# Low-rank attention and a maxout layer on one core: two heads of q fetched beside k, with E and F behind them, and batch 0's scores put ahead of v's projection

## The chip, the core and the metric

The kernel runs on one core of a Trainium2 chip. A core has a matrix engine (TensorE, PE in the profile), a vector engine (VectorE, DVE), an activation engine (ScalarE, ACT), a general engine (GpSimd, POOL) and a sequencer that issues transfers (SyncE, SP). Sixteen DMA engines move data between the chip's main memory (HBM) and the on-chip memory. A transfer is issued on a queue: SP's and ScalarE's are hardware queues, POOL's is a software queue. In this kernel every transfer that turns float32 into float16 on its way is on POOL's queue. TensorE writes into eight banks of accumulator memory (PSUM), and VectorE and ScalarE copy from there.

The metric is the device time of one execution in microseconds.

## The reference

The inputs are q, k and v with 8 batches, 8 heads, 1024 positions and 64 features per head, all float32; E and F, 64 by 1024; and three weight matrices. Keys and values are first projected from 1024 positions to 64:

```python
k_proj = np.einsum('ks,bhsd->bhkd', E, k)
v_proj = np.einsum('ks,bhsd->bhkd', F, v)
scores = (1.0 / np.sqrt(64)) * np.matmul(q, k_proj.transpose(0, 1, 3, 2))
attn = softmax(scores)                     # over the 64 projected keys
x = np.matmul(attn, v_proj)                # then heads side by side: 8192 x 512
h1 = x @ w1                                # 512 x 1024
h2 = x @ w2
out = np.maximum(h1, h2) @ w_out           # 1024 x 512, float32
```

The kernel computes the maximum as a ReLU of `x @ (w1 - w2)` plus `x @ w2`, and folds `w2 @ w_out` into one matrix m.

## The kernel before

**Steady state.** A batch is handled in two halves of its positions (`units`, 16 in all). For batches 1 to 7 the large products are done by a scheme with seven block products in place of eight (`up_steps`, L693, and `down_steps`, L785), with the sums and differences of blocks made on VectorE. The attention of a later batch is woven between them. All of it is an order written out by hand: a list `slots` of closures, and a table `steps` that hangs further closures on slots. The framework adds the semaphores and, under `manual_schedule`, leaves the order as written: each engine works through its own instructions in program order, so an instruction that waits holds up all behind it on the same engine.

**The beginning, where the change is.** Before that list, batch 0 is handled by straight-line code (L897 to L943), and the transfers for it are issued at the top:

- SP's queue: E (L80), the first two heads of k uncast in float32 (`kf_sb`, L81), F (L82). E and F share `ef_sb`.
- POOL's queue, in float16: heads 2 and 3 of k, then q's heads 0 to 3, k's 4 to 7, q's 4 to 7 (the double loop around L112), v in four pairs of heads (L117), then the weights w1 and w2 in pieces (L124, L133) and w_out (L137). The identity matrix is made on POOL after the first of them.
- `kf_sb` lies in the buffer that w_out takes later (tag `wo`). VectorE casts head 0 from it (L901) and ScalarE head 1 (L902).

The steps of batch 0, in the order that TensorE gets them: `step_eft` transposes E or F (L161, eight float32 transposes) and copies the result to `eft` (L167). `step_kv` projects k or v (L187): k four heads at a time into `kp`, v two or four heads at a time into `vp`. `step_kpt` transposes the projected k (L277). `step_qt` transposes four heads of q for one half of the positions (L303) and VectorE copies them (L308). `step_sc` makes the scores of a group of four heads (`g`) and a half (`j`) with 16 matmuls (L332), and ScalarE takes the exponential (L372). `step_dn` sums the exponentials with a matmul by ones (L344) and ScalarE takes the logarithm (L380); `step_inv` turns it into the reciprocal (L384). `step_at` multiplies by the projected v (L344 again) and VectorE scales the result into `xt` (L399). `step_wd` makes `w1 - w2` (L495). Then the first `up` products of batch 0 follow (L479), and from there the list of slots.

Between these steps stand `warm(n)`: n dummy matmuls of 128x512 ones (L147) whose results nobody reads.

`mm_bank()` hands out four PSUM banks in rotation unless a bank is named, and every `warm`, `step_kv`, `step_qt` and so on takes the next; `att_banks()` hands out two pairs of banks. The seven block products that make m (`m_steps`, L581) name banks 2 and 3 for themselves, at the end of batch 0's `up`, and `p5` there keeps a sum in bank 3.

Of the kernel before, what the change touches and what calls it, by code (L numbers as in the profile page):

```python
# [8 lines left out]
FP32 = mybir.dt.float32  # L9
# [7 lines left out]
def kernel(  # L17
# [12 lines left out]
    nc = tc.nc  # L30
# [5 lines left out]
    NC = S // 128  # L36
# [36 lines left out]
    def big(n, dtype=FP16):  # L73
        return const.tile([128, 16384 // mybir.dt.size(dtype) // 2], dtype, tag=f"big{n}", name=f"big{n}")

    ef_sb = big(0, FP32)[0:KP, :].rearrange("k (i s) -> k i s", i=2)
    kf_sb = const.tile([128, 2048], FP32, tag="wo", name="kf_sb")[:, 0 : 2 * NC * D].rearrange(
        "p (h c d) -> p h c d", h=2, d=D
    )
    nc.sync.dma_start(out=ef_sb[:, 0, :], in_=E)  # L80
    nc.sync.dma_start(out=kf_sb, in_=k[0, 0:2].rearrange("h (p c) d -> p h c d", c=NC))  # L81
    nc.sync.dma_start(out=ef_sb[:, 1, :], in_=F)  # L82
    nc.scalar.add_instruction(
        mybir.InstLoadActFuncSet(
# [16 lines left out]
    def load(t, n, src, b, h0, h1):  # L101
        nc.gpsimd.dma_start(  # L102
            out=t[n][:, h0:h1],
            in_=src[b, h0:h1].rearrange("h (p c) d -> p h c d", c=NC),
        )
# [3 lines left out]
        alloc(tiles[0], n)  # L109
    for h0 in (0, H // 2):  # L110
        for n, src in (("k", k), ("q", q)):
            load(tiles[0], n, src, 0, h0 + 2 * ((h0, n) == (0, "k")), h0 + H // 2)  # L112
            if (h0, n) == (0, "k"):
                ident = const.tile([128, 128], FP32)
                make_identity(nc, ident)
# [28 lines left out]
    def warm(n, att=False):  # L144
        w_ps = att_banks()[:, 0, :] if att else mm_bank()
        for _ in range(n):
            nc.tensor.matmul(  # L147
                out=w_ps, lhsT=ones16[:, 0:128], rhs=ones16, start=True, stop=True
            )

    warm(8)
    ident16 = const.tile([128, 128], FP16)
    nc.vector.tensor_copy(out=ident16, in_=ident)

# [3 lines left out]
    def step_eft(i):  # L158
        eft_ps = mm_bank()
        for c in range(NC):  # L160
            nc.tensor.transpose(  # L161
                out=eft_ps[:, c * KP : (c + 1) * KP],
                in_=ef_sb[:, i].rearrange("k (p c) -> k c p", c=NC)[:, c, :],
                identity=ident[:KP, :KP],
            )
        eng = nc.scalar.copy if i else nc.vector.tensor_copy
        eng(out=eft[i].rearrange("p c k -> p (c k)"), in_=eft_ps)  # L167
# [9 lines left out]
    def step_kv(t, h0=0, h1=H, which="kv", att=False, dma=False, copy=nc.vector.tensor_copy):  # L177
        kv_ps = att_banks()[:, 0, :] if att else mm_bank(n=0 if dma else None)
        n = (h1 - h0) * D
        both = which == "v"  # L180
        nh = 2 if both else h1 - h0
        for h in range(0, h1 - h0, nh):
            for c in range(NC):
                for w in which:
                    i = "kv".index(w)
                    for r in range(2) if both else (i,):
                        nc.tensor.matmul(  # L187
                            out=kv_ps[r * KP : (r + 1) * KP, h * D : (h + nh) * D],
                            lhsT=eft[i][:, c, :],
                            rhs=t[w][:, h0 + h : h0 + h + nh, c, :],  # L190
                            start=(c == 0), stop=(c == NC - 1),
                        )
        zd = lambda ap: ap.rearrange("p (h d z) -> p h z d", d=D // 2, z=2)
        if "k" in which:
            eng = nc.vector.tensor_copy if which == "k" or dma else nc.scalar.copy
            kp = t["kp"][:, h0:h1]
            eng(out=kp[:, :, 0, :], in_=kv_ps[0:KP, 0:n].rearrange("p (h d) -> p h d", d=D))
        if both:
            copy(out=t["vp"][:, h0:h1], in_=zd(kv_ps[:, 0:n]))
        elif "v" in which:  # L200
            def finish_v():
                nc.vector.tensor_copy(out=t["vp"][KP:128, h0:h1], in_=zd(kv_ps[KP:128, 0:n]))
                if dma:
                    nc.vector.tensor_copy(out=kp[:, :, 1, :], in_=kp[:, :, 0, :])
                    step_kpt_dma(t)
                else:
                    step_vp(t, h0, h1)

            if att:
                return finish_v  # L210
            finish_v()
# [149 lines left out]
    def new_xt(t):  # L361
        t["xt"] = xpool.tile([128, NP2, 2, HALF], FP16, tag="xt", name="xt_sb")
# [5 lines left out]
    def step_sc(t, g, j):  # L368
        sc_ps = att_banks()
        t["ps", g, j] = sc_ps  # L370
        score(t, g, j, [sc_ps[:, e, :] for e in range(2)])
        nc.scalar.activation(out=t["ex", g, j], in_=sc_ps, func=ACTF.Exp, scale=scale)  # L372

    def step_dn(t, g, j):
        dn_ps = t.pop(("ps", g, j))[:, :, 0:W]
        sums_into(t, g, j, dn_ps)
        ld = (ppool.tile([128, 2, W], FP32, tag="pd", bufs=4, name="ld_sb") if t is tiles[0]
              else soft.tile([128, 2, W], FP32, tag="soft", name="ld_sb"))
        t["ld", g, j] = ld
        nc.scalar.activation(out=t["ld", g, j], in_=dn_ps, func=ACTF.Ln)  # L380

    def step_inv(t, g, j):
        ld = t["ld", g, j]
        nc.scalar.activation(out=ld, in_=ld, func=ACTF.Exp, scale=-1.0)  # L384
# [178 lines left out]
    def m_steps():  # L563
        st = {}
        two = lambda ap: ap.rearrange("q (i m) -> q i m", i=2)

        def product(k, name, n):
            if n is not None:
                st[name] = mm_bank(n=n)
            bank = st[name]  # L570
            Bb = lambda h, c: wo_sb[:, h * NG : (h + 1) * NG, c * CH : (c + 1) * CH]
            T = lambda i: T_sb[:, i, 0:NG, :]
            a, w_ = {
                1: lambda: (m_blk(0, 0), Bb(0, 0)), 2: lambda: (m_blk(0, 1), Bb(1, 0)),
                3: lambda: (m_sums[3], Bb(1, 1)), 4: lambda: (m_blk(1, 1), T(3)),
                5: lambda: (m_sums[0], T(0)), 6: lambda: (m_sums[1], T(1)),
                7: lambda: (m_sums[2], T(2)),
            }[k]()
            for i in range(2):
                for c in range(NG):  # L580
                    nc.tensor.matmul(  # L581
                        out=bank[:, i * CH : (i + 1) * CH],
                        lhsT=a[:, c, i * 128 : (i + 1) * 128],
                        rhs=w_[:, c, :],
                        start=(n is not None and i == 0 and c == 0),
                        stop=(c == NG - 1), skip_group_check=True,
                    )
            return bank

        def block(j, c):  # L590
            return m_sb[:, 2 * j : 2 * j + 2, c * CH : (c + 1) * CH]

        def add(j, c, x, y):
            nc.vector.tensor_tensor(out=block(j, c), in0=two(x), in1=two(y), op=ALU.add)

        def p1():
            st["s1"] = keep("pu", product(1, "X", 2))

        def p2():
            add(0, 0, product(2, "Y", 3), st["s1"])  # L600

        def p6():
            st["u1"] = keep("pu", product(6, "X", None))

        def p5():
            st["s5"] = keep("pu", product(5, "Z", 3))

        def p7():
            st["u2"] = keep("pu", product(7, "X", None))

        def p3():
            add(0, 1, product(3, "Z", None), st["u1"])
            add(1, 1, st["u2"], st["s5"])

        def p4():
            nc.scalar.copy(out=block(1, 0), in_=two(product(4, "X", None)))

        return [p1, p2, p6, p5, p7, p3, p4]
# [46 lines left out]
    def keep(tag, bank, copy=nc.scalar.copy):  # L665
        x = ppool.tile([128, 512], FP32, tag=tag, bufs={"pu": 3, "pd": 4}[tag], name="p_sb")
        copy(out=x, in_=bank)  # L667
        return x
# [228 lines left out]
    t = tiles[0]  # L897
    new_attn(t)
    new_xt(t)
    step_eft(0)  # L900
    nc.vector.tensor_copy(out=t["k"][:, 0], in_=kf_sb[:, 0])  # L901
    nc.scalar.copy(out=t["k"][:, 1], in_=kf_sb[:, 1])  # L902
    warm(5)
    step_kv(t, 0, 4, "k")
    step_eft(1)
    step_kpt(t, 0, 4)
    warm(3)
    step_qt(t, 0, 4, 0, NI // 2)
    step_qt(t, 0, 4, NI // 2, NI)
    warm(2)  # L910
    step_sc(t, 0, 0)
    step_sc(t, 0, 1)
    warm(2)
    step_kv(t, 4, 8, "k")
    step_dn(t, 0, 0)
    warm(2)
# [1 line left out]
    step_dn(t, 0, 1)  # L918
    step_inv(t, 0, 0)
    step_inv(t, 0, 1)  # L920
    warm(2)
    step_qt(t, 4, 4, 0, NI // 2)
    step_qt(t, 4, 4, NI // 2, NI)
    warm(2)
    step_sc(t, 1, 0)
    step_kv(t, 0, 2, "v")
    step_sc(t, 1, 1)
    step_kv(t, 2, 4, "v")
    step_dn(t, 1, 0)
    step_dn(t, 1, 1)  # L930
    step_inv(t, 1, 0)
    step_inv(t, 1, 1)
    step_at(t, 0, 0)
    step_at(t, 0, 1, between=lambda: step_wd(0, 0, 2))
    step_kv(t, 4, 8, "v", True, copy=nc.scalar.copy)
    step_at(t, 1, 0, True)
    u0, u1 = [*up_slots(t, 0)], [*up_slots(t, 1)]
    step_wd(0, 2, 4)
# [207 lines left out]
```

## Time and profile before

| what | value |
|---|---|
| median of 3 runs | 320.87 us (320.71 to 320.96) |
| the profiled execution | 321.09 us, span 319.3 us |
| TensorE busy | 312.9 us, 98% of the span |
| VectorE busy | 241.3 us, 76% |
| ScalarE busy | 205.8 us, 64% |
| GpSimd busy | 39.7 us, 12% |
| TensorE busy in 1.40 to 24.00 us | 20.80 of 22.60 us |
| TensorE busy in 24.00 to 45.00 us | 20.94 of 21.00 us |
| TensorE busy in 45.00 to 100.00 us | 54.90 of 55.00 us |
| TensorE busy in 100.00 to 314.00 us | 214.00 of 214.00 us |
| first `up` product (L479) begins | 23.48 us |

The span runs from the first to the last instruction; the device time has some 1.8 us around it. A line of the timeline gives the start, the duration, the engine, the source line, the operation, what is written from what, how many instructions were merged into the line, and in square brackets how long the engine had been idle before it and what ended that. A line of the chain of waits gives start, duration, and what the end of the program waited for in that stretch. A line of a DMA queue gives packets, megabytes written and the time that the packets took, as a share of sixteen engines over the stretch. Dummy matmuls count as busy time of TensorE.

### The profile page before, as it was taken

To read this page: it belongs to the slowest core of one execution; us is meant where nothing else is said; L and a number is where in the kernel's file an instruction comes from. 1 tells how busy PE (TensorE), PEld (TensorE's weight loads), DVE (VectorE), ACT (ScalarE), POOL (GpSimd) and SP (SyncE) were. 2 spreads that over 40 slices of the span, in tenths; PEclk is the share of its full clock that TensorE was granted. 3 is DMA by queue.
4 is the path that set the end of the run, shared out by engine and by line. 5 is a ranking of instruction groups with operands and counts; after the bars stand their busy time and mean duration, and the time that the engine had idled before them with its cause. 6 is when DMAs were issued, how large, how long until landed. Compare 5 with 4: busy or idle time off the path is not lost.

```text
span 319.3 us, 9176 instructions
## 1 busy us (share of the span) xinstructions
PE 312.9 (98%) x3920; PEld 253.2 (79%) x3920; DVE 241.3 (76%) x434; ACT 205.8 (64%) x372; POOL 39.7 (12%) x63
## 2 busy tenths in 40 slices
PE   8989999999999999999999999999999999999996
PEld 3554588788887888788887888788887888888885
DVE  2356889787969696896969696996969696969683
ACT  2376742767776777477776777477776777765541
POOL 8269102003000300021000400030000000000000
PEclk9999999999999999999999999999999999999999
DMA  7999999999979899899999999889969231303124
GB/s 185 200 200 193 199 207 202 207 165 154 206 136 179 156 205 245 219 192 158 233 204 215 168 216 245 198 157 169 239 141 211 50 102 35 101 33 102 35 99 131
DMA packets 76424, 53.41 MB, mean 167 GB/s; under 512 B 29536, under 2 KB 76000, under 8 KB 76384
## 3 DMA queue, kind: packets, MB, share of 16 engines
q0 software_dynamic: 30688, 28.05, 56.2%
q1 hardware_dynamic: 45408, 24.58, 32.3%
q8 instruction: 30, 0.49, 0.6%
q10 hardware_dynamic: 288, 0.20, 0.2%
q14 instruction: 10, 0.08, 0.1%
HBM read 57.15 MB, written 16.78 MB: 232 GB/s over the span
## 4 chain that ended last, share of the span: by engine, by line
PE 92%; DMA 4%; ACT 1%; POOL 1%; DVE 1%; issue 0%; POOLq 0%; DVEq 0%
PE mm_ps L785 46%; PE mm_ps L693 27%; PE mm_ps L479 4%; DMA v_sb<-in_v_dram 4%; PE att_ps L344 3%; PE mm_ps L187 3%; PE mm_ps L332 3%; PE mm_ps L581 2%; PE att_ps L229 1%; PE mm_ps L303 1%; POOL k_sb L102 0%; POOL q_sb L102 0%; PE att_ps L504 0%; PE att_ps L332 0%; ACT ld_sb L384 0%
## 5 line engine op out<-in xcount | busy, mean ns | idle before, releaser
L667 ACT COPY p_sb<-mm_ps 128x512 f32<-128x512 f32 x179 | 101.7, 592 | 49.4 <-PE mm_ps L693 27.3
L785 PEld LDWEIGHTS <-big 128*128 128x128 f16 x768 | 73.5, 98 | 11.8 <-issue 3.6
L785 PE MATMUL mm_ps<-T_sb,big 128*128 128x256 f16 x576 | 77.0, 273 | 0.0
L708 DVE TENSOR_TENSOR gt_sb<-mm_ps,p_sb 128x512 f16<-128x512 f32 x56 | 38.5, 687 | 42.7 <-PE mm_ps L693 42.3
L693 PE MATMUL mm_ps<-big,big 128*128 128x256 f16 x336 | 50.4, 273 | 0.0
L693 PEld LDWEIGHTS <-big 128*128 128x128 f16 x448 | 43.8, 98 | 5.1
L785 PE MATMUL mm_ps<-wo_sb,gt_sb 128*128 128x256 f16 x256 | 42.8, 273 | 0.0
L785 PEld LDWEIGHTS <-gt_sb 128*128 128x128 f16 x376 | 35.6, 98 | 7.0 <-issue 3.0
L425 ACT ACTIVATE ex_sb<-mm_ps 128x512 f16<-128x512 f32 x50 | 27.2, 596 | 18.2 <-PE mm_ps L332 13.0
L693 PEld LDWEIGHTS <-wd_sb 128*128 128x128 f16 x336 | 32.9, 98 | 4.1
L693 PE MATMUL mm_ps<-xt_sb,wd_sb 128*128 128x256 f16 x224 | 33.0, 272 | 0.0
L454 DVE TENSOR_TENSOR xt_sb<-att_ps,ld_sb 128x1024 f16<-128x1024 f32 x26 | 31.7, 1218 | 0.2
L785 PE MATMUL mm_ps<-m_sb,xt_sb 128*128 128x256 f16 x128 | 24.4, 273 | 0.0
L711 DVE TENSOR_SCALAR gt_sb<-gt_sb 128x512 f16<-128x512 f16 (+1 forms) x60 | 22.7, 378 | 2.1
L815 DVE TENSOR_TENSOR o_sb<-mm_ps,p_sb 128x512 f32<-128x512 f32 x32 | 21.8, 682 | 2.8 <-ACT p_sb L839 2.0
L295 POOL COPY junk<-qt_sb 1x1 f16<-1x1 f16 x6 | 1.1, 177 | 176.2 <-DMA qt_sb<-q_sb 176.2
L653 DVE TENSOR_TENSOR big<-gt_sb 128x1024 f16<-128x1024 f16 x32 | 21.9, 683 | 0.0
L785 PE MATMUL mm_ps<-wo_sb,big 128*128 128x256 f16 x128 | 21.5, 273 | 0.0
L754 ACT ACTIVATE gt_sb<-mm_ps 128x512 f16<-128x512 f32 x28 | 16.8, 601 | 5.7 <-PE mm_ps L693 5.7
L785 PE MATMUL mm_ps<-T_sb,gt_sb 128*128 128x256 f16 x120 | 20.3, 273 | 0.0
L785 PEld LDWEIGHTS <-xt_sb 128*128 128x128 f16 x188 | 18.4, 98 | 2.1
L708 DVE TENSOR_TENSOR gt_sb<-p_sb 128x512 f16<-128x512 f32 x28 | 19.1, 682 | 0.7 <-ACT p_sb L667 0.6
(112 smaller groups left out, 434.7 us busy)
## 6 DMA issues: line engine op xcount, KB each, us to landing
out_dram<-o_sb SPq DMA_DIRECT2D x62, 256.0 KB, 2.7
k_sb<-in_k_dram POOLq DMA_DIRECT2D x7, 1024.0 KB, 10.4
v_sb<-in_v_dram POOLq DMA_DIRECT2D x7, 1024.0 KB, 17.0
q_sb<-in_q_dram POOLq DMA_DIRECT2D x5, 1024.0 KB, 23.9
q_sb<-in_q_dram POOLq DMA_DIRECT2D x6, 512.0 KB, 16.2
big<-in_moe_w_dram POOLq DMA_DIRECT2D x12, 128.0 KB, 6.3
v_sb<-in_v_dram POOLq DMA_DIRECT2D x4, 256.0 KB, 13.8
wo_sb<-in_moe_w_out_dram POOLq DMA_DIRECT2D x1, 1024.0 KB, 10.4
```

The lines of the kernel that those rows point to most:

```text
L187: nc.tensor.matmul(out=kv_ps[r * KP : (r + 1) * KP, h * D : (h + nh) * D], lhsT=eft[i][:, c, :], rhs=t[w][:, h0 + h : h0 + h + nh, c, :], ...
L425: nc.scalar.activation(out=t["ex", g, j][:, e, :], in_=banks[e], func=ACTF.Exp, scale=scale)
L454: nc.vector.tensor_tensor(out=x_out(t, g, j).rearrange("q z o n -> q o z n"), in0=at_ps.rearrange("q o (z n) -> q o z n", z=2), in1=ld[:, ...
L479: nc.tensor.matmul(out=h_ps, lhsT=wd_sb[:, r, fb * 128 : (fb + 1) * 128], rhs=t["xt"][:, r, :, j * W : (j + 1) * W], start=(r == 0), stop= ...
L653: nc.vector.tensor_tensor(out=S(i), in0=S(0) if x is None else x, in1=y(), op=op)
L667: copy(out=x, in_=bank)
L693: nc.tensor.matmul(out=bank[:, m * W : (m + 1) * W], lhsT=w_[:, n_, (2 * d + m) * 128 : (2 * d + m + 1) * 128], rhs=a[:, n_, :], start=(n ...
L708: nc.vector.tensor_tensor(out=c_blk(j, c), in0=two(x), in1=two(y), op=ALU.add)
L711: nc.vector.tensor_scalar_max(ap, ap, 0.0)
L754: nc.scalar.activation(out=out, in_=in_, func=ACTF.Relu)
L785: nc.tensor.matmul(out=bank[i][:, 0:CH] if two_banks else bank[:, i * CH : (i + 1) * CH], lhsT=a(c)[:, i * 128 : (i + 1) * 128], rhs=w_(c) ...
L815: nc.vector.tensor_tensor(out=o_sb, in0=two(x), in1=two(y), op=ALU.add)
```

## The change

The first two heads of q are fetched like those of k: uncast, in float32, by a hardware queue, into the other half of the same buffer (`raw_sb`, now 128 by 2048), and cast on chip, head 1 on ScalarE and head 0 on VectorE. k's two heads become the first transfer on SP's queue, q's two the first on ScalarE's, ahead of its table load. E and F follow k on SP. POOL's second transfer shrinks to q's heads 2 and 3. The casts now stand ahead of E's transposes in the code, so on VectorE the two casts come before the copy of E's transposes.

On TensorE the four scores steps of batch 0 keep their order, but scores (1,1) move ahead of v's first projection, and the values of group 0 move ahead of the denominators (1,1). v's last four heads are projected after those denominators, as before, but on ScalarE the copy of that projection now stands between the two reciprocals. The dummies go from 8, 5, 3, 2, 2, 2, 2, 2 to 10, 4, 2, 2, 1, 2. With two `warm` calls fewer the rotation of banks is shifted by two, and `p5` of `m_steps` names bank 1 in place of 3.

```diff
     ef_sb = big(0, FP32)[0:KP, :].rearrange("k (i s) -> k i s", i=2)
-    kf_sb = const.tile([128, 2048], FP32, tag="wo", name="kf_sb")[:, 0 : 2 * NC * D].rearrange(
-        "p (h c d) -> p h c d", h=2, d=D
+    raw_sb = const.tile([128, 2048], FP32, tag="wo", name="raw_sb").rearrange(
+        "p (n h c d) -> p n h c d", n=2, h=2, d=D
     )
+    for n, (queue, src) in enumerate(((nc.sync, k), (nc.scalar, q))):
+        queue.dma_start(out=raw_sb[:, n], in_=src[0, 0:2].rearrange("h (p c) d -> p h c d", c=NC))
     nc.sync.dma_start(out=ef_sb[:, 0, :], in_=E)
-    nc.sync.dma_start(out=kf_sb, in_=k[0, 0:2].rearrange("h (p c) d -> p h c d", c=NC))
     nc.sync.dma_start(out=ef_sb[:, 1, :], in_=F)
...
-            load(tiles[0], n, src, 0, h0 + 2 * ((h0, n) == (0, "k")), h0 + H // 2)
+            load(tiles[0], n, src, 0, h0 + 2 * (h0 == 0), h0 + H // 2)
...
-    warm(8)
+    warm(10)
...
-            st["s5"] = keep("pu", product(5, "Z", 3))
+            st["s5"] = keep("pu", product(5, "Z", 1))
...
     new_xt(t)
+    for n, name in enumerate("kq"):
+        nc.scalar.copy(out=t[name][:, 1], in_=raw_sb[:, n, 1])
+        nc.vector.tensor_copy(out=t[name][:, 0], in_=raw_sb[:, n, 0])
     step_eft(0)
-    nc.vector.tensor_copy(out=t["k"][:, 0], in_=kf_sb[:, 0])
-    nc.scalar.copy(out=t["k"][:, 1], in_=kf_sb[:, 1])
-    warm(5)
+    warm(4)
     step_kv(t, 0, 4, "k")
     step_eft(1)
     step_kpt(t, 0, 4)
-    warm(3)
     step_qt(t, 0, 4, 0, NI // 2)
     step_qt(t, 0, 4, NI // 2, NI)
     warm(2)
     step_sc(t, 0, 0)
     step_sc(t, 0, 1)
-    warm(2)
     step_kv(t, 4, 8, "k")
     step_dn(t, 0, 0)
     warm(2)
...
-    warm(2)
+    warm(1)
     step_qt(t, 4, 4, 0, NI // 2)
     step_qt(t, 4, 4, NI // 2, NI)
     warm(2)
     step_sc(t, 1, 0)
+    step_sc(t, 1, 1)
     step_kv(t, 0, 2, "v")
-    step_sc(t, 1, 1)
     step_kv(t, 2, 4, "v")
     step_dn(t, 1, 0)
+    step_at(t, 0, 0)
+    step_at(t, 0, 1, between=lambda: step_wd(0, 0, 2))
     step_dn(t, 1, 1)
     step_inv(t, 1, 0)
+    step_kv(t, 4, 8, "v", True, copy=nc.scalar.copy)
     step_inv(t, 1, 1)
-    step_at(t, 0, 0)
-    step_at(t, 0, 1, between=lambda: step_wd(0, 0, 2))
-    step_kv(t, 4, 8, "v", True, copy=nc.scalar.copy)
     step_at(t, 1, 0, True)
```

## The prediction

> **What bounds the kernel now.** I read the page first (shares of the engines, slices), then the waits of TensorE by stretch, then the chain of waits over the first 27 us, then the timeline of that stretch, then the DMA queues second by second.
>
> The page says that TensorE is the bound and that the clock is granted in full in every slice:
>
> ```profile
> PE 312.9 (98%) x3920; PEld 253.2 (79%) x3920; DVE 241.3 (76%) x434; ACT 205.8 (64%) x372; POOL 39.7 (12%) x63
> PEclk9999999999999999999999999999999999999999
> ```
>
> By stretch (busy time of each engine between given times) TensorE is busy 20.94 of 21.00 us from 24 to 45, 54.90 of 55.00 from 45 to 100 and 214.00 of 214.00 from 100 to 314. Nothing of the diff adds work there, so whatever moves the first `up` product (L479), which starts at 23.48 us, moves the end by the same amount. Only 1.4 to 24 us has slack: 20.80 of 22.60 us busy, dummy products (L147) included. The chain that ended last, in order of time, shows what holds L479 there:
>
> ```profile
> 4.84 13.53 DMA v_sb<-in_v_dram
> 18.37 0.04 issue
> 18.41 0.64 PE mm_ps L187 x16
> 19.05 0.39 PE att_ps L332 x16
> 19.44 0.02 issue
> 19.46 1.02 ACT ex_sb L372
> 20.49 1.02 ACT ld_sb L380 x2
> 21.50 1.04 ACT ld_sb L384 x2
> 22.54 0.27 ACT vp_sb L199
> 22.81 0.04 issue
> 22.86 0.63 PE att_ps L344 x32
> 23.49 1.90 PE mm_ps L479 x8
> ```
>
> Two things meet: the transfers (v's first pair of heads lands at 18.37) and, behind it, the softmax of the second group. Ahead of that lies a front chain (E, k's projection, q's transposes, scores), in the timeline:
>
> ```profile
> 1.46 3.60 PE L147 MATMUL mm_ps<-ones 128*128 128x512 f16 x8 [1.46 <-DVE ones L140]
> 4.99 1.10 PE L161 MATMUL mm_ps<-ident,big 64*128 64x64 f32 x8
> 6.02 1.25 PE L147 MATMUL mm_ps<-ones 128*128 128x512 f16 x5
> 7.28 1.06 PE L187 MATMUL mm_ps<-k_sb,eft 128*64 128x256 f16 x8
> 8.27 1.09 PE L161 MATMUL mm_ps<-ident,big 64*128 64x64 f32 x8
> 10.76 1.07 PE L303 MATMUL mm_ps<-ident,q_sb 128*128 128x128 f16 x16 [0.40 <-DMA q_sb<-in_q_dram]
> 16.32 1.06 PE L303 MATMUL mm_ps<-ident,q_sb 128*128 128x128 f16 x16
> 18.41 0.64 PE L187 MATMUL mm_ps<-v_sb,eft 128*64 128x128 f16 x16 [0.26 <-DMA v_sb<-in_v_dram]
> ```
>
> See that q's first transposes wait for q (10.76), and that eight dummies take 3.60 us (0.45 each) while five later ones take 1.25 (0.25 each). So the array runs slow at first, although the page's clock row shows nothing of it.
>
> **The change, part by part.** Times are on the profiled execution's span.
>
> *E comes later: the cost.* E was the first DMA on SP (0.74, listed landing 4.0 us on, so 4.7). It now stands behind k's two heads, with q's two on ScalarE's queue beside them, so 1.05 MB go ahead of its 0.26 MB. No row shows two hardware queues together, so I bound it by the hardware queue's rows in one-microsecond windows: 0.19 MB in 2:3, 0.26 in 3:4, 0.32 in 4:5, and 0.26 in 71% of 6:7 (0.37 per us). That brings 0.77 MB by 5.0, the other 0.28 by 5.9, E's 0.26 by 6.6. kf's last bytes move at about 5.4 and it counts as landed at 5.9, so 0.4 to 0.5 more: E lands at 7.0. Ends: 6.5 (both queues at 0.37 from the start) and 8.3 (k's heads 2 and 3 from POOL's queue slip ahead of E; their 256 packets fill about 1.3 us of 5:7). The row nearest to E is kf, issued in the slot that E gets now (1.38), and it went ahead of those heads; hence 7.0. The dummies before it (10 at 0.43 to 0.45) end at 5.9, so TensorE idles about 1.1 us there.
>
> *The front chain from 7.0.* With the spacings of the timeline: E's eight transposes 1.03 (4.99 to 6.02), their copy 0.69 and 0.1 of hand-over, so k's projection at 8.9 (the 4 dummies, 0.85, end then too) against 7.28. Next F's transposes +0.99 = 9.9, kp's +1.02 = 10.9, +0.25 q's at 11.15: no 3 dummies and no wait there now. The scores follow 1.43 later, 12.6 against 12.19. Then k's heads 4 to 7: 13.5 against 13.64, as 2 dummies (0.45) and a DMA wait (0.42) are gone. From there to q's second transposes were 2.46 (first weight load at 16.10); minus one dummy, 15.9. Scores (1,0) at 17.35 against 17.74, and (1,1) right behind, when DVE has copied the second half: 17.95 against 18.98.
>
> New waits in it. The casts of k and q (ScalarE 0.62 each, DVE 0.50 each) stand ahead of E's copy on DVE; from a landing at 6.3 they end by 7.6, E's transposes at 8.05, so they are hidden unless q's two heads land after 6.9. k's heads 2 and 3 land some 1.3 behind E's bytes (8.3; needed 8.9), F 9.0 (needed 9.9), q's heads 2 and 3 10.2 (needed 11.4). ScalarE's DMA issue (0.57, as on SP) goes before its table load of 1.28, and ScalarE has nothing until 5.9.
>
> *v and the second group.* Scores (1,1) no longer stand behind v's first pair. The pairs follow, 0.57 each: 18.35 and 18.95. Group 0's values came 1.33 after the second pair's start (19.32 to 20.65) because the denominators (1,1) waited for ScalarE (0.35). Those are behind now, so 1.0 (the copy of vp ends 0.97 after that start): 19.95 against 20.65. Values 0.56 and denominators 0.25, then v's last four heads 20.8 against 21.21. There the last pair of v limits: POOL is released by it at 21.88 and TensorE ran into its half of the work at about 21.75, so it landed about 21.7. Half of 1.08 after that is 22.25, vp's copy 0.36 and hand-overs 0.1, values 0.63: `up` at 23.35 with v as before (-0.15). DVE is ready: its products start 0.6 earlier.
>
> *The transfers.* q's two heads leave the software queue (256 packets at 195 to 200 per us: -1.3 us) and come as 256 hardware packets of 2 KB (125 to 160 per us in 3:5: +1.6 to +2.05, or, at E's and F's 0.37 MB per us, +1.4). Against that, the half-empty 2:3 (80%) and q's slow begin (151 packets in 7:8 where 195 are usual, 0.2 us) now overlap with k's. Net from -0.4 to +0.75. I take -0.15, as F's rate is the nearest row of a queue that runs full: v's last pair at 21.55, `up` at 23.2, and the front chain (20.8 + 1.08 + 0.46 + 0.63 = 22.97) just keeps up.
>
> *Order and banks later.* Two fewer rotations of four mean that m's first products use the banks of the last two `up` blocks. The evictions of those end at 39.40 and 40.26; the products start at 39.46 and 0.87 later. Cost 0 to 0.2, taken as 0. The product kept in bank 1 is read out by 45.96, and its next user starts at 47.0: nothing. Five dummies fewer (26 to 21) lie in waits or are counted above. POOL's issue of q (0.77) only gets shorter; w is queued behind v and comes with it.
>
> Sum: -0.15 (v's path freed) -0.15 (transfers) = -0.3. The profiled run took 321.09 with a span of 319.3, 0.22 over the median of the runs shown; so 320.8 for it, and 320.6 for the median.
>
> [...] In 5:6 the software queue moved 183 packets and the hardware queue only 20, though F had been issued at 2.00: F waited until k's heads were through, then went ahead of q. [...]
>
> **Rivals.**
> 1. *E waits behind POOL's k* (8.3). F's row speaks for it, kf's against. k's projection at 10.2, scores (1,1) at 19.2, all behind 1.3 later than above: v's last heads at 22.1, plus 1.08, 0.46 and 0.63 `up` at 24.3, +0.8: 321.7 (320.9 to 322.0). It decides as soon as E lands after 7.5, where the chain costs what it did before; slower by my bound from 8.15 on.
> 2. *The clock falls or rises late.* TensorE idles from 5.9 to E. Eight matmuls (0.11 apart) and four dummies (0.21) at half speed cost 1.7: 321.9. Against it: the rate had risen by 6.02, after 4.5 us without a pause. [...]
> 3. *v lands no earlier, or later* by up to 0.3: 320.7 to 321.0. The change is hidden by the transfers. For it: the same engines carry the same bytes from HBM.
> 4. *The transfers gain more* (-0.4, and v's first pair, which landed 2.4 after q's last half where 1.3 is its size, keeps step): `up` at 22.7 to 22.85, -0.65 to -0.8: 320.1. Against it: the front chain must then have E by 6.6.
>
> **How the numbers follow.** Forecast 0.37 (own range 320.2 to 321.0), rival 1 0.25, rival 2 0.07, rival 3 0.13, rival 4 0.18. A measurement of this kernel tells 0.2% (0.64 us) from nothing. Faster by that: rival 4 and a tail of the forecast, 0.22. Slower: rival 2, three quarters of rival 1, and 0.05 for costs after 24 us that the timeline doesn't show: 0.31. The rest, 0.47, is within. The range leaves one in ten on each side: 320.0 (rival 4) to 321.9 (rivals 1 and 2).
>
> **What will show it.** E's transposes at 7.0; q's first transposes at 11.2 without a DMA wait; scores (1,1) ahead of v at 18.0; first L479 at 23.2; TensorE without a wait after it. E's transposes at 8 or later mean rival 1; matmuls 0.21 apart after 7 us rival 2; v's last pair at 21.7 rival 3. I am wrong if `up` starts outside 22.9 to 24.0, or if the shift is not passed on to the end.

## The result, and the profile after

The changed kernel takes 322.83 us (median of 7 runs, 322.1 to 323.85), the kernel before 320.96 beside it (7 runs, 320.7 to 321.7): a ratio of 1.0057, with an interval of 1.0037 to 1.0076. The change costs about 1.9 us, where 0.3 us of gain was forecast. The time lies above the range of the forecast (320.0 to 321.9); what rival 2 named, a late or falling clock, is what the profile shows.

The profiled execution took 322.28 us, with a span of 320.5. Two lines of the page, in the same order as before: busy time by engine, and the granted clock in 40 slices of the span.

```profile
PE 313.0 (98%) x3915; PEld 253.5 (79%) x3915; DVE 239.8 (75%) x435; ACT 206.2 (64%) x373; POOL 40.6 (13%) x63
PEclk9799999999999999999999999999999999999999
```

TensorE is as busy as before. One digit differs, the 7 in the second slice of 8 us: there the clock was not granted in full. The timeline of TensorE in the beginning (start, duration, engine, line, operation, count, idle time ahead of it):

```profile
1.46 4.18 PE L148 MATMUL mm_ps<-ones 128*128 128x512 f16 x10 [1.46 <-DVE ones L141]
7.77 1.11 PE L162 MATMUL mm_ps<-ident,big 64*128 64x64 f32 x8 [2.12 <-DMA big<-in_E_dram]
8.81 1.89 PE L148 MATMUL mm_ps<-ones 128*128 128x512 f16 x4
10.63 1.75 PE L188 MATMUL mm_ps<-k_sb,eft 128*64 128x256 f16 x8
12.31 1.09 PE L162 MATMUL mm_ps<-ident,big 64*128 64x64 f32 x8
13.57 1.07 PE L304 MATMUL mm_ps<-ident,q_sb 128*128 128x128 f16 x16
...
20.37 0.41 PE L333 MATMUL att_ps<-qt_sb,kpt_sb 64*32 64x256 f16 x16 [0.16 <-DVE qt_sb L309]
20.71 1.08 PE L188 MATMUL mm_ps<-v_sb,eft 128*64 128x128 f16 x32
...
22.85 1.08 PE L188 MATMUL att_ps<-v_sb,eft 128*64 128x128 f16 x32
24.41 0.63 PE L345 MATMUL att_ps<-ex_sb,vp_sb 64*32 64x256 f16 x32 [0.48 <-ACT vp_sb L200]
25.01 1.90 PE L480 MATMUL mm_ps<-xt_sb,wd_sb 128*128 128x512 f16 x8
```

(Lines of the changed kernel are one higher than before: L480 is L479.) Three things are to be seen. E's transposes wait 2.12 us for E and start at 7.77 where 7.0 was forecast. Behind them the four dummies take 1.89 us and the eight matmuls of k's projection 1.75, where before they took 0.25 each and 1.06: the array runs at half speed. And the first `up` product starts at 25.01, 1.53 later than before. v's projection (20.71 and 22.85) no longer waits for a transfer.

Busy time by stretch (length, busy time and count of PE, PEld, DVE, ACT and POOL, granted clock, share of the DMA engines, GB/s) shows the clock itself:

```profile
5.00:8.60 3.60, 1.48 (x11) 0.86 (x9) 0.85 (x2) 1.18 (x2) 2.67 (x4) 1.00 1.13 230
8.70:12.00 3.30, 3.30 (x13) 1.58 (x12) 0.69 (x1) 0.00 (x0) 1.43 (x2) 0.50 1.24 206
12.10:15.00 2.90, 2.90 (x37) 2.17 (x34) 1.47 (x4) 0.59 (x1) 0.71 (x1) 1.00 1.24 206
```

From 8.70 to 12.00 the clock is 0.50, ahead of it and behind it 1.00; its records put the fall at 8.66 and the rise at 12.07. The stretch ahead of the fall is the one in which TensorE worked 1.48 of 3.60 us. The chain that ended last starts with E, and every piece of the slow stretch lies on it:

```profile
1.26 6.38 DMA big<-in_E_dram
7.63 0.14 issue
7.77 1.11 PE mm_ps L162 x8
8.88 1.82 PE mm_ps L148 x4
10.70 1.68 PE mm_ps L188 x8
12.38 1.02 PE mm_ps L162 x8
13.40 0.24 PE mm_ps L278 x8
13.64 0.57 PE mm_ps L304 x8
```

The seven runs fall into three groups by their mean granted clock: 0.995 with 322.1 to 322.28 us (three runs, the profiled one among them), 0.988 with 322.83 and 322.89, and 0.999 with 323.59 and 323.85. Only the first group has a profile, so where the clock was slow in the other four runs, the median among them, is not shown.

### The profile page after: what moved, and what is told of

It is laid out like the page before. It is cut to its first block, busy times and chain, and to the rows that moved or that the text cites. A ratio compares the mean times of both kernels' runs of the same rounds, so it can differ in the third digit from the quotient of the medians.

```text
span 320.5 us, 9170 instructions
## 1 busy us (share of the span) xinstructions
PE 313.0 (98%) x3915; PEld 253.5 (79%) x3915; DVE 239.8 (75%) x435; ACT 206.2 (64%) x373; POOL 40.6 (13%) x63
## 4 chain that ended last, share of the span: by engine, by line
PE 95%; DMA 2%; DVE 1%; ACT 0%; issue 0%; SPq 0%; DVEq 0%
PE mm_ps L786 46%; PE mm_ps L694 27%; PE mm_ps L480 4%; PE mm_ps L188 4%; PE att_ps L345 3%; PE mm_ps L333 2%; DMA big<-in_E_dram 2%; PE mm_ps L582 2%; PE att_ps L230 1%; PE mm_ps L304 1%; PE mm_ps L148 1%; DVE qt_sb L309 1%; PE mm_ps L162 1%; PE att_ps L333 1%; PE att_ps L505 0%; PE mm_ps L345 0%
## 5 line engine op out<-in xcount | busy, mean ns | idle before, releaser
L296 POOL COPY junk<-qt_sb 1x1 f16<-1x1 f16 x6 | 2.2, 362 | 173.1 <-DMA qt_sb<-q_sb 173.1
L712 DVE TENSOR_SCALAR gt_sb<-gt_sb 128x512 f16<-128x512 f16 (+1 forms) x60 | 20.9, 348 | 2.1
L755 ACT ACTIVATE gt_sb<-mm_ps 128x512 f16<-128x512 f32 x28 | 16.8, 601 | 5.7 <-PE mm_ps L694 5.7
```

Source lines behind the costliest of these rows:

```text
L712: nc.vector.tensor_scalar_max(ap, ap, 0.0)
L755: nc.scalar.activation(out=out, in_=in_, func=ACTF.Relu)
```

## The experiments

The theories: **A**, the pause of TensorE ahead of E takes the clock down or keeps it from rising; **B**, E's lateness alone costs the time; **C**, the new order of the steps costs it.

**More dummies, same transfers** (A against B: E lands as late).

```diff
-    warm(10)
+    warm(20)
```

> The changed kernel with 20 dummy matmuls ahead of E's transposes where it has 10; nothing else differs, and E's transfer is untouched. Theory A (the pause): TensorE's pause of 2.12 us ahead of E lets the clock fall (0.5 from 8.66 to 12.07 in the profile of the changed kernel), and this stretch costs about 1.6 us (four dummies 1.89 us in place of 0.85, eight matmuls 1.75 in place of 1.06). Then without the pause k's projection starts at 8.9 to 9.1 in place of 10.63, the first up product at 23.3 to 23.6 in place of 25.01, and the time is 320.6 to 321.1, without the spread of 322.1 to 323.85. Theory B (E alone): E's transposes at 7.77 in place of 4.99 cost the time, whatever the clock does: 322 to 324, as the changed kernel. Theory C (the new order of the steps costs the time): as B.

Measured: 321.0 us (320.75 to 321.56), ratio 0.9996 to the kernel before (0.9972 to 1.002). 1.8 us are gone with ten dummies that compute nothing. In the profile:

```profile
1.46 7.04 PE L148 MATMUL mm_ps<-ones 128*128 128x512 f16 x20 [1.46 <-DVE ones L141]
8.43 1.09 PE L162 MATMUL mm_ps<-ident,big 64*128 64x64 f32 x8
9.46 1.04 PE L148 MATMUL mm_ps<-ones 128*128 128x512 f16 x4
10.43 1.06 PE L188 MATMUL mm_ps<-k_sb,eft 128*64 128x256 f16 x8
```

E's transposes start 0.66 *later* than in the changed kernel, without a wait, and k's projection still starts 0.2 earlier, as it runs at full speed. A holds; B falls as the main cause. `up` starts at 24.12 in this profile, later than the 23.3 to 23.6 that A had, as twenty dummies are longer than E needs; the profiled run took 321.43 us.

**E ahead of k on SP's queue** (does an early E cure it?).

```diff
+    nc.sync.dma_start(out=ef_sb[:, 0, :], in_=E)
     for n, (queue, src) in enumerate(((nc.sync, k), (nc.scalar, q))):
...
-    nc.sync.dma_start(out=ef_sb[:, 0, :], in_=E)
...
-    warm(10)
+    warm(8)
...
+    step_eft(0)
     for n, name in enumerate("kq"):
...
-    step_eft(0)
-    warm(4)
+    warm(5)
```

> The changed kernel with E back at the head of SP's queue, k's and q's two heads behind and beside it, F last; the casts behind E's copy, and 8 and 5 dummies as before. All else is the changed kernel's. Theory A: E's transposes start at 5.0, right behind the dummies, no slow stretch after it; k's projection waits for k's heads 2 and 3 (8.0 to 8.5) and the rest follows, first up product 23.2 to 23.6, time 320.5 to 321.1. Theory B: the same, since E is early. Theory C: 322 or more, because the order of the steps is still the new one. A time between 321.2 and 322 would say that k's later heads, pushed back by q's uncast ones, are a cost of their own.

Measured: 322.68 us (320.67 to 324.03), ratio 1.0047 (1.0019 to 1.0076); a miss. In the profile, which took 323.64:

```profile
1.46 3.60 PE L148 MATMUL mm_ps<-ones 128*128 128x512 f16 x8 [1.46 <-DVE ones L141]
5.93 1.12 PE L162 MATMUL mm_ps<-ident,big 64*128 64x64 f32 x8 [0.88 <-DMA big<-in_E_dram]
6.98 2.31 PE L148 MATMUL mm_ps<-ones 128*128 128x512 f16 x5
10.78 1.89 PE L188 MATMUL mm_ps<-k_sb,eft 128*64 128x256 f16 x8 [1.48 <-DMA k_sb<-in_k_dram]
12.60 1.14 PE L162 MATMUL mm_ps<-ident,big 64*128 64x64 f32 x8
13.67 0.42 PE L278 MATMUL mm_ps<-ident,kp_sb 64*64 64x64 f16 x8
14.02 1.89 PE L304 MATMUL mm_ps<-ident,q_sb 128*128 128x128 f16 x16
```

E came 1.8 earlier, but the pause only moved: 0.88 ahead of E and 1.48 ahead of k's heads 2 and 3, which now arrive last. The array stays slow through q's transposes (1.89 for 16, at full speed 1.07) and the dummies behind them, up to about 16.8 us; this trace holds no record of the clock, so the durations alone tell it. `up` starts at 26.46. Against the kernel with sixteen dummies (below) k's projection starts 0.89 later and `up` 2.78 later: the late k is a cost of its own, and about 1.9 us lie in the slow stretch behind it. So an early E alone doesn't cure it, as TensorE still runs dry for k.

**The order of the steps alone** (C): the kernel before, with only the order of scores, v's projections, values and denominators changed as in the diff.

```diff
     step_sc(t, 1, 0)
-    step_kv(t, 0, 2, "v")
     step_sc(t, 1, 1)
+    step_kv(t, 0, 2, "v")
     step_kv(t, 2, 4, "v")
     step_dn(t, 1, 0)
-    step_dn(t, 1, 1)
-    step_inv(t, 1, 0)
-    step_inv(t, 1, 1)
     step_at(t, 0, 0)
     step_at(t, 0, 1, between=lambda: step_wd(0, 0, 2))
+    step_dn(t, 1, 1)
+    step_inv(t, 1, 0)
     step_kv(t, 4, 8, "v", True, copy=nc.scalar.copy)
+    step_inv(t, 1, 1)
```

> The kernel before with the new order of the steps alone (scores (1,1) ahead of v, the values of group 0 ahead of the denominators (1,1), the copy of v's last heads between the two reciprocals); transfers and dummies as before. Theories A and B: the order costs nothing and gains up to 0.3 us, first up product at 23.2 to 23.5, time 320.5 to 321.0. Theory C: a loss of 1 us or more, 322.

Measured: 320.73 us (320.66 to 322.8), ratio 1.0002 (0.998 to 1.0024). In the profile `up` starts at 23.33, 0.15 ahead of before, as the first term of the sum had it; in the time it can't be told from nothing. C, which had 322, falls.

**The transfers alone**: the new loads and casts, with the order and the dummies of before.

```diff
...
+    for n, (queue, src) in enumerate(((nc.sync, k), (nc.scalar, q))):
+        queue.dma_start(out=raw_sb[:, n], in_=src[0, 0:2].rearrange("h (p c) d -> p h c d", c=NC))
     nc.sync.dma_start(out=ef_sb[:, 0, :], in_=E)
-    nc.sync.dma_start(out=kf_sb, in_=k[0, 0:2].rearrange("h (p c) d -> p h c d", c=NC))
...
-            load(tiles[0], n, src, 0, h0 + 2 * ((h0, n) == (0, "k")), h0 + H // 2)
+            load(tiles[0], n, src, 0, h0 + 2 * (h0 == 0), h0 + H // 2)
...
+    for n, name in enumerate("kq"):
+        nc.scalar.copy(out=t[name][:, 1], in_=raw_sb[:, n, 1])
+        nc.vector.tensor_copy(out=t[name][:, 0], in_=raw_sb[:, n, 0])
     step_eft(0)
-    nc.vector.tensor_copy(out=t["k"][:, 0], in_=kf_sb[:, 0])
-    nc.scalar.copy(out=t["k"][:, 1], in_=kf_sb[:, 1])
```

> The kernel before with the new transfers and casts alone (k and q uncast first, E and F behind); order of the steps and dummies as before (8, 5, 3, 2, 2, 2, 2, 2). Theory A: E's transposes at 7.7 again, and a pause of about 2.9 us ahead of them, since the dummies end at 4.9; the clock falls or never rises before 10: 1.5 to 3 us lost, 322.3 to 324. Theory B: 1.2 to 2 us lost from E alone, 322 to 323, with or without a slow stretch. Theory C: as the kernel before, 321.

Measured: 324.44 us (324.03 to 326.12), ratio 1.0108 (1.0076 to 1.0141), the slowest of all. With eight dummies the pause is 2.69:

```profile
1.46 3.60 PE L148 MATMUL mm_ps<-ones 128*128 128x512 f16 x8 [1.46 <-DVE ones L141]
7.75 1.11 PE L162 MATMUL mm_ps<-ident,big 64*128 64x64 f32 x8 [2.69 <-DMA big<-in_E_dram]
8.79 2.32 PE L148 MATMUL mm_ps<-ones 128*128 128x512 f16 x5
11.04 1.92 PE L188 MATMUL mm_ps<-k_sb,eft 128*64 128x256 f16 x8
```

Here the clock had not risen before the pause; it rose at 13.51, and `up` started at 27.20. The whole loss lies in the transfers with the pause that they bring; the change's other dummies and its new order of the steps together took back 1.6 us of it.

**E at the head of ScalarE's queue, ahead of q**, with 13 and 8 dummies, so that TensorE never pauses.

```diff
+    nc.scalar.dma_start(out=ef_sb[:, 0, :], in_=E)
...
-    nc.sync.dma_start(out=ef_sb[:, 0, :], in_=E)
...
-    warm(10)
+    warm(13)
...
+    step_eft(0)
     for n, name in enumerate("kq"):
...
-    step_eft(0)
-    warm(4)
+    warm(8)
```

> The changed kernel with E at the head of ScalarE's queue, ahead of q (k heads SP's, F behind it), the casts behind E's copy, 13 dummies at the start and 8 after E's transposes. E at 5.2 to 6, k's heads 2 and 3 on POOL's queue at 8.5 to 9.3 (9.3 in the changed kernel), k's projection at 9 to 9.5, and v's last pair 0.3 earlier than before. Theory A: with TensorE busy from 1.46 to 9 the clock is up by 8.3 at the latest; first up product 23.2 to 23.7, time 320.5 to 321.0. Theory B: E is early, so 320.5 to 321. If k's heads come at 10 or later, as when E stood ahead of k on SP's queue (10.7), 321.2 to 322.

Measured: 321.02 us (320.77 to 322.49), ratio 1.0 (0.9979 to 1.002). The profile has the clock up at 6.88, no pause ahead of E (7.03, right behind the dummies), and k's projection only at 9.89, `up` at 23.57. The 8.3 that A has, here and in two runs below, as the latest rise is the author's estimate, which no trace shows; beside the 6.88 here the rise lies at 7.50 with the order alone. Without a pause the new transfers cost nothing that the median shows; E's transposes, 0.7 earlier than in the changed kernel, bring no gain over the kernel before, with k's projection behind eight dummies. Two of the twelve runs, at 322.46 and 322.49 us, still have a mean granted clock of 0.994 and 0.995. Such runs occur in the kernel before too: beside these experiments 5 of its 110 took 322.7 to 324.4 us at 0.989 to 0.995. None of them has a profile.

**The pause without the transfers.** A control first: the kernel before, with the transposing transfers of batches 2 to 7 replaced by plain ones; then the same with three opening dummies in place of eight.

```diff
-        nc.sync.dma_start_transpose(
-            out=t["kpt"], in_=t["kp"].rearrange("p h r d -> p (h r d)")
-        )
+        for r in range(2):
+            nc.sync.dma_start(out=t["kpt"][r * D : (r + 1) * D], in_=t["kp"][:, :, r, :])
...
-        nc.sync.dma_start_transpose(
-            out=t["qt"][:, h0:h1].rearrange("q h (i p) -> q (h i) p", p=128),
-            in_=t["q"][:, h0:h1].rearrange("p h c d -> p (h c d)"),
+        nc.sync.dma_start(
+            out=t["qt"][:, h0:h1], in_=t["q"][:, h0:h1].rearrange("p h c d -> p h (c d)")
         )
```

> A control for the next two: the kernel before, but the transposing transfers of q and k in batches 2 to 7 (L289, L315) are plain copies of the same bytes, so those batches' q and k are used untransposed. The first 45 us hold no such transfer, so the first up product stands at 23.3 to 23.6; the time is within 1 us of the kernel before, 320 to 321.5, since TensorE has no wait after 24 us.

Measured: 321.05 us (320.82 to 321.26), ratio 0.9994 (0.9983 to 1.0005). It stands for the kernel before.

```diff
-    warm(8)
+    warm(3)
```

> The control with 3 dummy matmuls at the start where it has 8; transfers of batch 0, order and all else as in the kernel before, and with the control's plain copies in batches 2 to 7. E lands at 4.7 to 5.0 as before, so TensorE pauses from 2.9 to about 4.8, some 1.9 us, nearly the pause of the changed kernel. [...] Theory B (E's lateness alone costs the time): E is not late, so the control's time.

Measured: 321.4 us (321.05 to 322.92), 1.0015 to the kernel before (1.0001 to 1.0028), and 0.35 over the control, where the author's estimate for A was 1 to 3.5.

```profile
4.85 1.12 PE L161 MATMUL mm_ps<-ident,big 64*128 64x64 f32 x8 [1.93 <-DMA big<-in_E_dram]
5.90 2.31 PE L147 MATMUL mm_ps<-ones 128*128 128x512 f16 x5
```

The pause of 1.93 kept the clock down, as A has it: five dummies take 2.31 instead of 1.25, and the clock rises at 8.16, against 4.75 in the control. That is just ahead of k's projection, which runs at full speed (1.03), not at half as expected, so the slow stretch behind the pause costs only 1.06. And the control waits for k in that place:

```profile
7.80 1.03 PE L187 MATMUL mm_ps<-k_sb,eft 128*64 128x256 f16 x8 [0.62 <-DMA k_sb<-in_k_dram]
```

k's projection is then half a microsecond late (8.32 against 7.80), q's transposes too (11.21 against 10.69), and v's first projection, which waits 0.28 for v in the control, 0.17 (18.52 against 18.35); `up` starts at 23.60 against 23.54. So a pause alone is not the price: it costs what of the slow stretch lies on a chain without slack. In the control there are waits for transfers behind it, which take most of it up; in the changed kernel the chain runs from E to `up` without another transfer, so all of it shows.

**Order and dummies, without the transfers**: the control with 13 opening dummies, the three ahead of q's transposes gone, and the order above.

```diff
-    warm(8)
+    warm(13)
...
-    warm(3)
+    mm_bank()
```

> The control with the new order of the steps, 13 dummies at the start for 8, and none ahead of q's transposes for 3; transfers of batch 0 as before, and the control's plain copies in batches 2 to 7. E's transposes start between 5.9 and 7.0 in place of 5.0, which the wait for q hides (q's transposes at 10.8 to 11.2). Theory A: TensorE is busy without a gap from 1.46 to 7, so the clock is up by 8.3 in every run and slow runs disappear; first up product at 23.3, 0 to 0.4 us under the control's median. Theory B: the control's time or up to 1 us over it, as E's transposes come later.

Measured: 321.16 us (320.92 to 321.64), ratio 1.0005 (0.9994 to 1.0016); `up` at 23.62. No gain over the control; a miss.

**Sixteen dummies**, so that the pause is shorter without delaying E.

```diff
-    warm(10)
+    warm(16)
```

> The changed kernel with 16 dummies ahead of E's transposes where it has 10 (20 in the first experiment). They end between 6.7 and 8.3, so TensorE waits at most 1.1 us for E, which lands at 7.7. Theory A: the clock is up by 8.3 in nearly every run; this leaves E's own cost, first up product at 23.4 to 23.9, 320.7 to 321.1. Theory B: 322 to 324, as with 10 dummies, E being as late.

Measured: 320.73 us (320.51 to 321.05, 12 runs), ratio 0.9991 (0.998 to 1.0001), as A had it, though the pause is 1.53 and not 1.1 at most. The profile is of the slowest of them, 321.05:

```profile
1.46 4.93 PE L148 MATMUL mm_ps<-ones 128*128 128x512 f16 x16 [1.46 <-DVE ones L141]
7.93 1.07 PE L162 MATMUL mm_ps<-ident,big 64*128 64x64 f32 x8 [1.53 <-DMA big<-in_E_dram]
8.93 1.04 PE L148 MATMUL mm_ps<-ones 128*128 128x512 f16 x4
9.89 1.06 PE L188 MATMUL mm_ps<-k_sb,eft 128*64 128x256 f16 x8
...
23.68 1.90 PE L480 MATMUL mm_ps<-xt_sb,wd_sb 128*128 128x512 f16 x8
```

The busy time in the same two stretches as above. This trace holds no record of the clock, so the 1.00 in the third column from the end says nothing here; that the array is at full speed behind the pause is told by the four dummies, 1.04 against 1.89, and by k's projection, 1.06 against 1.75.

```profile
5.00:8.60 3.60, 2.07 (x13) 1.13 (x12) 1.07 (x2) 1.24 (x2) 2.68 (x4) 1.00 1.13 245
8.70:12.00 3.30, 3.30 (x29) 2.31 (x30) 1.11 (x2) 0.00 (x0) 1.43 (x2) 1.00 1.24 206
```

This is the cleanest pair: the edit is six dummies and nothing else. E's transposes are 0.16 later than in the changed kernel and TensorE still pauses 1.53, but the array stays fast, and `up` starts 1.33 earlier. One thing besides the length of the pause differs in the two profiles: here the dummies' spacing halves at about 4.15, so the clock rose 1.1 earlier. That the array stays fast in the other runs too is read from their times, none of them above 321.05. Against the kernel before, E's 2.9 us of lateness cost 0.2 at `up` (23.68 against 23.48) and nothing in the time.

**F's transposes in two halves, in place of dummies** (more slack for the front chain, on top of the sixteen dummies). Left out below: `step_eft` takes a range of blocks, and two calls of `mm_bank()` keep the rotation of the banks.

```diff
...
     step_kv(t, 0, 4, "k")
-    step_eft(1)
     step_kpt(t, 0, 4)
...
-    warm(2)
+    step_eft(1, 0, NC // 2)
     step_sc(t, 0, 0)
...
     step_dn(t, 0, 0)
-    warm(2)
+    step_eft(1, NC // 2, NC)
     step_kpt(t, 4, 8)
...
```

> The changed kernel with 16 dummies at the start, and F's eight transposes in two halves of four, each in the place of two dummies (behind q's first transposes, and behind the first denominators), in place of all eight between k's projection and kp's transposes. Nothing is left out. With 16 dummies alone the first up product stood at 23.7 and the time at 320.73. Theory A (with the clock up, the front chain on TensorE sets the start of up): kp's transposes come 0.4 to 0.5 earlier, first up product at 23.1 to 23.4, 320.3 to 320.6. Rival (v's transfers set it): 23.6 and 320.7 as before.

Measured: 320.76 us (320.32 to 320.9), ratio 0.999 (0.9981 to 1.0). The chain that ended last no longer goes through E:

```profile
10.71 12.18 DMA big<-in_moe_w_dram
22.88 0.03 issue
22.91 0.02 DVEq L502
22.93 0.04 issue
22.98 0.43 DVE wd_sb L502
23.41 0.05 issue
23.46 1.90 PE mm_ps L486 x8
```

With the front chain out of the way the first weights, queued on POOL behind v, hold `up` at 23.46 (23.1 to 23.4 had been expected), and the time is that of sixteen dummies alone. That is where a faster front stops paying.

**F on ScalarE's queue behind q**, with sixteen dummies, and then **both**.

```diff
-    nc.sync.dma_start(out=ef_sb[:, 1, :], in_=F)
+    nc.scalar.dma_start(out=ef_sb[:, 1, :], in_=F)
```

> The changed kernel with 16 dummies at the start and F issued on ScalarE's queue behind q, so that nothing follows E on SP's. Theory A with E's lateness as the rest of the loss: if F's packets slowed E down (E's and F's took 0.17 to 0.30 us each side by side, 0.16 in the kernel before), E's transposes start 0.2 to 0.5 earlier than 7.9, first up product 23.2 to 23.5, 320.3 to 320.7. If F has no part in it, E at 7.7 to 7.9 again and 320.7. With F ahead of E's end on the other queue E could also come later, by up to 0.4.

> The two runs before this one together. If both gains are on the same chain they add up until v's last pair limits at 23.0: first up product 23.0 to 23.3, 320.1 to 320.5. If v limits at once, the better of the two.

Measured: 322.15 us (320.93 to 323.67), ratio 1.005 (1.0032 to 1.0069), for F on ScalarE's queue; 321.67 (320.6 to 323.85), ratio 1.0024 (1.0001 to 1.0048), with the halves as well; both are misses. The two profiles are of runs near the fastest (320.93 and 320.66), with the clock up at 6.47 and 6.31 and `up` at 23.62 and 23.37. E's transposes start at 7.96 and 8.00, against 7.93 with F behind E, so F's packets did not hold E up. The runs 1 to 3 us above have no profile. All eight above 323 us have a mean granted clock of 0.989 to 0.995, and one stretch of 3.41 us at 0.50 gives 0.995, as in the profile of the changed kernel; so the clock was down in them for such a stretch or more. Where in the span, and why F's place should bring it, stays open.

## Why the prediction was wrong, point by point

**The order of the steps: right, and too small to matter.** -0.15 at `up` was forecast and 0.15 came (23.33 against 23.48) with the order alone.

**E's landing: mis-sized.** 7.0 was forecast, 7.63 measured. The queue order was right: k's two heads, then E, with POOL's k behind it (9.3). The two hardware queues had moved 0.22, 0.62, 1.04 and 1.28 MB by 3, 4, 5 and 6 us. Sixteen packets of 4 bytes close each transfer on SP's queue in the traces; E's lie at 5.69 to 6.64, so its last bytes passed at about 6.6, as forecast. What failed is the term "0.4 to 0.5 more" between the last bytes and the landing, taken from kf. For E it is 1.0, and before it was 1.1 (closing packets by 3.65, listed landing 4.7). E's own row was there to read it from. E's place behind POOL's k, for which F's row spoke in the trace of before, did not come: the first bytes of E moved at 4.9, of POOL's k at 5.35. Rival 1's place (E at 8 or later) was missed, but its limit of 7.5 was passed.

**The pause: twice as long as counted.** 1.1 us became 2.12: 0.77 from E (0.63 in the landing, 0.14 from there to the first transpose), and 0.25 as the ten dummies were over at 5.64 and not at 5.9.

**The clock: the step that failed.** The sum put the pause's effect on the clock at nothing; measured, the clock fell behind it and cost 1.64 us on the chain to `up`. Rival 2 had the right price, 1.7, and 0.07 of the chance. Four dummies took 1.89 instead of 0.85 to 1.04, eight matmuls 1.75 instead of 1.06. The argument against it ran from the rate at 6.02 in the trace of before, which said that the clock would be up, and it was (5.25); but that trace has no pause of more than 0.4 us between 1.46 and 22 us, so it could say nothing of a fall. That a pause of 1.1 us costs nothing was the author's estimate, which the trace of before does not show; the runs show no fall behind 1.22 (F in halves) and 1.53 us (sixteen dummies), and the fall behind 2.12. In the changed kernel's records the clock is 1.00 from 5.25 to 8.66 and 0.50 from there to 12.07, 3.41 us each. The first of the two stretches was not idle: TensorE worked 1.28 us in it, 0.39 on dummies and 0.89 on E's transposes, and the clock fell all the same.

**The front chain's spacings: right.** From F's transposes to scores (1,1) 8.05 us were forecast (9.9 to 17.95) and 8.06 measured (12.31 to 20.37); from v's last heads to `up`, where the front chain sets it, 2.17 (20.8 to 22.97) and 2.16 (22.85 to 25.01). Between them, scores (1,1) to v's last heads, 2.48 were enough where 2.85 had been counted. Scores (1,1) ran ahead of v without a wait. So the front chain's 22.97 became 25.01: +0.77 from E, +1.64 from the clock, -0.37 here.

**The transfers' -0.15: did not show.** POOL's wait for v's last pair ended at 21.82 against 21.88 before. In no profile did `up` start before 23.3. In the kernel with F in halves v's last product starts at 20.89 and is stretched to 1.37, where it takes 1.08 with v there, and then the weights behind v hold `up` at 23.46. Rival 3, that v lands no earlier, was right on this term.

**The shift passed on: mostly.** 1.53 at `up` became 1.2 in the span. From `up` to the end all these profiles have between 295.4 and 295.8 us, before 295.8, after 295.5, and the transfers with the old order 295.5 too. Where in the steady part these tenths go was not followed.

**With the clock held, the number comes close, but not by the forecast's path**: 320.73 us for sixteen dummies against 320.6 forecast. What the forecast missed is in the main one effect, and six dummies undo it. But `up` stands at 23.68 in that profile, inside the forecast's 22.9 to 24.0 and not at its 23.2, so the gain of 0.3 that the forecast added up is not shown, and that the times agree is in part luck. What the other transfers bring is then about 0.1% and may be nothing (0.9991 and 0.999, with intervals from 0.998 to 1.0001 and 0.9981 to 1.0). No version beats the kernel before by a clear margin.

## What to carry to other kernels

In this kernel a transfer that was moved back in the beginning cost more than its own delay, because TensorE ran dry for it: the clock fell (0.50 from 8.66 to 12.07 in the changed kernel), or was not yet up (until 13.51 with the transfers alone), and the work behind the pause ran at half speed (four dummies in 1.89 us, which take 1.04 at full speed; five in 2.32, which took 1.25 before). How much of that shows depends on the waits behind it. Lay the opening dummies out to the latest landing of what they wait for, read that landing from the same transfer's own row (listed landing against the window in which its bytes moved), and look at the clock by stretch, not by the mean over the span, which hid 1.6 us in 0.995. And a trace without a pause says nothing on what a pause does.

## What the runs showed of the hardware that was not expected

*The clock fell behind a pause with work on both sides of it.* In the changed kernel the pause ahead of E is 2.12 us. TensorE worked 1.28 of the 3.41 us from the rise at 5.25 on, the clock fell at 8.66, and the four dummies behind E's transposes took 1.89. With a pause of 1.53 (sixteen dummies) or 1.22 (F in halves) the same four took 1.04, so no fall. In both the clock was also up earlier: at about 4.15 by the spacing of the dummies, and at 4.32 by the record. Where it was not yet up ahead of the pause, it came late. With the transfers alone the pause is 2.69 and the rise comes at 13.51; with the pause alone it is 1.93, and the rise comes at 8.16 where the control has it at 4.75; with E ahead of k there are two, 0.88 and 1.48, and the durations show a slow array up to about 16.8. How long a pause may be, and how much work beside it holds the clock, is not shown: no profile has the clock up ahead of a pause between 1.53 and 2.12 us, and no run was made to test it.

*The same beginning meets the clock differently from run to run.* Three kernels with the same work on TensorE up to 6 us had the rise at 5.91 (before), 4.75 (the control) and 7.50 (order alone). The changed kernel's runs spread over 1.75 us, those with sixteen dummies over 0.54. That the moment of the rise makes the difference between the changed kernel's runs is the author's estimate; only one of them has a profile.

*The clock row is silent until the first change.* In the changed kernel, as before, it shows 1.00 while the opening dummies take 0.42 us each, where four at full speed take 1.04 together; only the durations of equal matmuls tell that the array is still slow there. Two of the traces, E ahead of k and sixteen dummies, hold no record of the clock at all and show 1.00 throughout, though the first is slow for some 15 us.

*Not tried:* E on ScalarE's queue beside k with q left on POOL's, the pause alone in the kernel before without the replaced transfers, and a profile of one of the runs above 322 us with F on ScalarE's queue.
